# Attention then mixture of experts on one core: the first q and k turned on TensorE, later q loads in pieces between units, ten units held for the tail

## The chip, the cores and the metric

The kernel runs on one core of a Trainium2 chip. The time is the device time of one execution in microseconds (us), the median of three: 524.33 us before (523.4 to 526.0). The profile is of one further execution, whose span is 527.4 us. A core has five engines with a queue each: TensorE (PE, with its weight loads shown apart as PEld), VectorE (DVE), ScalarE (ACT), GpSimd (POOL) and SyncE (SP), which here only issues transfers. ScalarE and GpSimd issue transfers too.

## The reference

Eight sequences of 384 tokens go through multi-query attention (16 heads of 64, one shared k and v), and the result x (3072 tokens of 1024) through a mixture of 16 experts in 4 groups, where each token takes the best group and in it the best expert.

```python
scores = scale * q @ k.T                     # (8, 16, 384, 384)
attn = exp(scores - max) / sum
x = (attn @ v).transpose(0, 2, 1, 3).reshape(8 * 384, 16 * 64)
g_idx = argmax(x @ w_group); e_idx = argmax(x @ w_expert[g_idx])
out = g_w * e_w * (relu(x @ w1[g, e]) @ w2[g, e])   # g_w, e_w: softmax weights of the chosen
```

All is float32 outside; the experts' matmuls run in bfloat16. The kernel loads for each sequence the expert that most of its first 128 tokens choose, computes all 384 tokens with it, and treats tokens that chose another expert at the end, in the tail: here a single further (sequence, expert) pair, whose at most 128 tokens are gathered, computed and scattered over the output.

## The kernel before

The order of instructions on each engine is the order in the program. A step p is a third of a sequence's queries (128 rows, 16 heads); there are 24. `side` gives one of three PSUM buffers that the scores, the expert units and the small matmuls share.

```python
def load_q(b):
    t = pool.tile([P, HP, NB, 32], FP32, tag="qraw", bufs=2, name="qraw")
    for a in range(2):
        for j in range(2):
            nc.sync.dma_start(out=t[64 * a + 32 * j:64 * a + 32 * j + 32].rearrange("p h k d -> p (h k) d"), in_=qv[b, a, j].rearrange("i h k d -> i (h k) d"))
    q_raw[b] = t

def load_q_first():
    t = pool.tile([P, HP, P // 32, 32], FP32, tag="presum", bufs=2, name="qfirst")
    for k in range(P // 32):
        for a in range(2):
            for j in range(2):
                (nc.sync if a == 0 or k == 0 else nc.scalar).dma_start(out=t[64 * a + 32 * j:64 * a + 32 * j + 32, :, k], in_=qv[0, a, j, :, :, k])
    return t

def load_kv(b):
    kt = pool.tile([P, NB, 32], FP32, tag="k", bufs=1, name="k")
    for a in range(2):
        for j in range(2):
            (nc.scalar if b == 0 else nc.sync).dma_start(out=kt[64 * a + 32 * j:64 * a + 32 * j + 32], in_=kv[b, 0, j])
    k_raw[b] = kt
    vt = pool.tile([P, KB, D], FP32, tag="v", name="v")
    for c in range(2):
        (nc.gpsimd if b == 0 else nc.sync).dma_start(out=vt[64 * c:64 * c + 64], in_=v[b, 0].rearrange("(j i) d -> i j d", j=KB))
    v_sb[b] = vt
```

The first third of q is thus loaded twice: by `load_q_first` in small pieces and again with the whole of the first sequence. q and k are loaded so that a row's two halves of 32 lie on different partitions, and VectorE's 32x32 transpose finishes the turn:

```python
def prep_k(b):
    kT[b] = pool.tile([P, S], FP32, tag="kT", name="kT")
    nc.vector.transpose(out=kT[b][:], in_=k_raw[b][:].rearrange("p k d -> p (k d)"))

def q_of(p):
    b, st = divmod(p, ST)
    return q_raw[b][:, :, st * (P // 32):(st + 1) * (P // 32)].rearrange("p h k d -> p h (k d)")

def prep_q(p, src=None):
    qT[p] = pool.tile([P, 2 * CW], FP32, tag="qT", bufs=2, name="qT")
    dst = qT[p][:].rearrange("p (h n) -> p h n", h=HP)
    if src is None:
        nc.vector.transpose(out=dst, in_=q_of(p))
    else:
        for i in range(2):
            ns = slice(i * D, (i + 1) * D)
            nc.vector.transpose(out=dst[:, :, ns], in_=src[:, :, 2 * i:2 * i + 2].rearrange("p h k d -> p h (k d)"))

def scores(p, j):
    b = p // ST
    ps = side([P, 2, CW], FP32, "s")
    for c in range(2):
        for a in range(2):
            r = slice(64 * a, 64 * a + 64)
            nc.tensor.matmul(out=ps[64 * c:64 * c + 64, a, :], lhsT=kT[b][r, j * D:(j + 1) * D], rhs=qT[p][r, c * CW:(c + 1) * CW], start=True, stop=True)
    t = pool.tile([P, 2, CW], FP32, tag="pt", bufs=9, name="pt")
    nc.scalar.activation(out=t[:], in_=ps[:], func=ACTF.Exp, scale=scale)
    pt[p, j] = t
...
    def pre_add(p, j):      # sums of exponentials, VectorE
...
    def join(p):            # small matmuls: sums over keys
...
    def invert(p):          # reciprocal and spread, VectorE: rinv
...
    def weigh(p):           # xT = o * rinv on VectorE, bf16 copy on GpSimd; x_bf stored after a sequence
...
    def choose_a(b): ...    # logits of the first 128 tokens, VectorE
    def choose_b(b): ...    # counts, the expert's index, and the loads of its w1 and w2 (two buffers each)
```

The expert of a sequence is cut into 14 units that fill TensorE between the steps: 8 h units and 6 y units.

```python
    def h_unit(fc):
        if fc == 0:
            state["h"] = pool.tile([P, FO, S], BF16, tag="hT", bufs=1, name="hT")
        ps = side([P, CW], FP32, "hps")
        for ko in range(KO):
            nc.tensor.matmul(out=ps[:, 0:S], lhsT=w1[:, ko, fc * P:(fc + 1) * P], rhs=xb[:, ko, :], start=(ko == 0), stop=(ko == KO - 1))
        nc.scalar.activation(out=state["h"][:, fc, :], in_=ps[:, 0:S], func=ACTF.Relu)

    def y_unit(st, nh):
        cs = slice(nh * CW, (nh + 1) * CW)
        y = place(st, cs)
        ps = side([P, CW], FP32, "yps")
        for fo in range(FO):
            nc.tensor.matmul(out=ps[:], lhsT=state["h"][:, fo, st * P:(st + 1) * P], rhs=w2[:, fo, nh * CW:(nh + 1) * CW], start=(fo == 0), stop=(fo == FO - 1))
        nc.scalar.activation(out=y, in_=ps[:], func=ACTF.Copy, scale=gs_of()[:, st:st + 1])
        store(st, cs, y)
...
def first_units(b):
    def place(st, cs):
        y = pool.tile([P, CW], FP32, tag="y", bufs=3, name="y")
        return y[:]

    def store(st, cs, y):
        nc.sync.dma_start(out=outv[b, :, st, cs], in_=y)
    return moe_units(wts[b][0], wts[b][1], xbf[b], lambda: gsel[b], place, store)
```

The loop over the steps:

```python
def phase(n, jobs):
    for i in range(n):
        fill(1)
        if i > 0 and jobs:
            jobs.pop(0)()
    while jobs:
        jobs.pop(0)()

def jobs_choose(b):
    return [lambda: gate_a(b, 0, 1), lambda: choose_a(b), lambda: choose_b(b)]

def jobs_gate(b):
    return [lambda: gate_a(b, 1, ST), lambda: gate_math(b, gate_logits(gate_b(b))), lambda: gate_c(b)]
...
for p in range(NP):
    b, st = divmod(p, ST)
    jobs = {2: jobs_choose(0), 4: jobs_gate(0)}.get(p, [])
    for j in range(3):
        scores(p, j)
    if 0 < p < NP - 1:
        prep_q(p + 1)
    for j in range(KB):
        if p > 0:
            values(p - 1, j)
        if j == 1 and p > 0:
            join(p - 1)
        if j + 3 < KB:
            scores(p, j + 3)
        if 0 < j < 4 and jobs:
            jobs.pop(0)()
        if j > 0:
            pre_add(p, j)
        if j == 1 and p > 0:
            invert(p - 1)
        if j == 3:
            stats_q(p)
            if st == 0 and b + 1 < B:
                load_q(b + 1)
    assert not jobs
    if p == 0:
        prep_q(1)
    if p > 0:
        weigh(p - 1)
    fold_keys(p)
    if st == 1 and b + 1 < B:
        load_kv(b + 1)
    if st == 2 and b + 1 < B:
        prep_k(b + 1)
        stats_k(b + 1)
    if p > ST:
        jobs = []
        if st == 1:
            jobs = jobs_choose(b)
        if st == 0 and b > 1:
            jobs = jobs_gate(b - 1)
        if p == NP - 1:
            jobs = [bound_a, bound_b]
        phase(4 if st == 0 else 5, jobs)

    join(NP - 1)
    for j in range(KB):
        values(NP - 1, j)
    invert(NP - 1)
    weigh(NP - 1)
    fill(2)
    gate_a(last, 1, ST)
    fill(1)
    ... # gate, index of the further pair, fills between
    _, w1c, w2c, xe, ge = load_pair(pair0)      # 7 fills stand before this
    ... # gather of its tokens, 13 fills between
    while begun[0] < B or units:
        fill(1)
    ... # ph = w1c, xc -> hc (ACT); py = hc, w2c -> yc (ACT); scatter
```

Of the kernel before, what the change touches and what calls it, by code (L numbers as in the profile page):

```python
# [9 lines left out]
FP32 = mybir.dt.float32  # L10
BF16 = mybir.dt.bfloat16
I32 = mybir.dt.int32
U32 = mybir.dt.uint32
P = 128
# [7 lines left out]
def kernel(  # L22
# [11 lines left out]
    nc = tc.nc  # L34
# [7 lines left out]
    ST = S // P  # L42
# [32 lines left out]

    q_raw, k_raw, v_sb, kT, qT, pt, xT, xbf, gsel, wts = {}, {}, {}, {}, {}, {}, {}, {}, {}, {}

    def load_q(b):
        t = pool.tile([P, HP, NB, 32], FP32, tag="qraw", bufs=2, name="qraw")
        for a in range(2):  # L80
            for j in range(2):
                nc.sync.dma_start(out=t[64 * a + 32 * j:64 * a + 32 * j + 32].rearrange("p h k d -> p (h k) d"), in_=qv[b, a, j].rearrange("i h k d -> i (h k) d"))
        q_raw[b] = t

    def load_q_first():
        t = pool.tile([P, HP, P // 32, 32], FP32, tag="presum", bufs=2, name="qfirst")
        for k in range(P // 32):
            for a in range(2):
                for j in range(2):
                    (nc.sync if a == 0 or k == 0 else nc.scalar).dma_start(out=t[64 * a + 32 * j:64 * a + 32 * j + 32, :, k], in_=qv[0, a, j, :, :, k])  # L90
        return t

    def load_kv(b):
        kt = pool.tile([P, NB, 32], FP32, tag="k", bufs=1, name="k")
        for a in range(2):
            for j in range(2):
                (nc.scalar if b == 0 else nc.sync).dma_start(out=kt[64 * a + 32 * j:64 * a + 32 * j + 32], in_=kv[b, 0, j])
        k_raw[b] = kt
        vt = pool.tile([P, KB, D], FP32, tag="v", name="v")
        for c in range(2):  # L100
            (nc.gpsimd if b == 0 else nc.sync).dma_start(out=vt[64 * c:64 * c + 64], in_=v[b, 0].rearrange("(j i) d -> i j d", j=KB))
        v_sb[b] = vt

    def load_w1(w1, e):
        for a in range(2):
# [7 lines left out]
        nc.tensor.matmul(out=warm[:, 0:P], lhsT=ones_bf[:], rhs=ones_bf[:], start=True, stop=True)  # L113
    ident = singles.tile([P, P], FP32, name="ident")
    make_identity(nc, ident)
    load_kv(0)
    q_first = load_q_first()
    load_q(0)

    one = singles.tile([P, 1], FP32, name="one")  # L120
    nc.vector.memset(one[:], 1.0)
    iota16 = singles.tile([P, GE], FP32, name="iota16")
    nc.gpsimd.iota(iota16[:], pattern=[[1, GE]], base=0, channel_multiplier=0, allow_small_or_imprecise_dtypes=True)
    iota128 = singles.tile([P, NPAIR], FP32, name="iota128")
# [45 lines left out]

    def stats_k(b):
        junk = pool.tile([P, 2 * CW], BF16, tag="junk", bufs=1, name="junk")
        nc.scalar.activation(out=junk[:, 0:S], in_=k_raw[b][:].rearrange("p k d -> p (k d)"), func=ACTF.Square, accum_out=stat_k[:, b:b + 1])

    def prep_k(b):
        kT[b] = pool.tile([P, S], FP32, tag="kT", name="kT")
        nc.vector.transpose(out=kT[b][:], in_=k_raw[b][:].rearrange("p k d -> p (k d)"))

    def q_of(p):
        b, st = divmod(p, ST)  # L180
        return q_raw[b][:, :, st * (P // 32):(st + 1) * (P // 32)].rearrange("p h k d -> p h (k d)")

    def prep_q(p, src=None):
        qT[p] = pool.tile([P, 2 * CW], FP32, tag="qT", bufs=2, name="qT")
        dst = qT[p][:].rearrange("p (h n) -> p h n", h=HP)
        if src is None:
            nc.vector.transpose(out=dst, in_=q_of(p))  # L187
        else:
            for i in range(2):
                ns = slice(i * D, (i + 1) * D)  # L190
                nc.vector.transpose(out=dst[:, :, ns], in_=src[:, :, 2 * i:2 * i + 2].rearrange("p h k d -> p h (k d)"))

    def scores(p, j):
        b = p // ST
# [10 lines left out]

    def pre_add(p, j):
        if j == 1:
            presum[p] = pool.tile([P, 2, CW], FP32, tag="presum", bufs=2, name="presum")
            nc.vector.tensor_add(out=presum[p][:], in0=pt[p, 0][:], in1=pt[p, 1][:])  # L209
        else:  # L210
            nc.vector.tensor_add(out=presum[p][:], in0=presum[p][:], in1=pt[p, j][:])  # L211
# [133 lines left out]
    def moe_units(w1, w2, xb, gs_of, place, store):  # L345
# [24 lines left out]
                units.append(lambda st=st, nh=nh: y_unit(st, nh))  # L370
        return units

    def first_units(b):
        def place(st, cs):
            y = pool.tile([P, CW], FP32, tag="y", bufs=3, name="y")
            return y[:]

        def store(st, cs, y):
            nc.sync.dma_start(out=outv[b, :, st, cs], in_=y)
        return moe_units(wts[b][0], wts[b][1], xbf[b], lambda: gsel[b], place, store)  # L380

    NP = B * ST

    prep_k(0)
    for _ in range(36):
        nc.tensor.matmul(out=warm[:, 0:P], lhsT=ones_bf[:], rhs=ones_bf[:], start=True, stop=True)
    prep_q(0, q_first)
    load_gw()
    stats_k(0)

    units = []
    begun = [0]
# [1 line left out]
    def fill(n):  # L394
        while n > 0:
            if not units:
                if begun[0] >= B or begun[0] not in wts:
                    return
                units.extend(first_units(begun[0]))
                begun[0] += 1  # L400
            units.pop(0)()
            n -= 1

    def phase(n, jobs):
        for i in range(n):
            fill(1)
            if i > 0 and jobs:
                jobs.pop(0)()
        while jobs:
# [7 lines that stand above are left out]
# [10 lines left out]
    def bound_b():  # L427
# [9 lines left out]
        nc.vector.tensor_copy(out=oki[:], in_=okf[:])  # L437
        bound["okf"] = okf

    for p in range(NP):  # L440
        b, st = divmod(p, ST)
        jobs = {2: jobs_choose(0), 4: jobs_gate(0)}.get(p, [])
        for j in range(3):
            scores(p, j)
        if 0 < p < NP - 1:
            prep_q(p + 1)
        for j in range(KB):
            if p > 0:
                values(p - 1, j)
            if j == 1 and p > 0:  # L450
                join(p - 1)
            if j + 3 < KB:
                scores(p, j + 3)
            if 0 < j < 4 and jobs:
                jobs.pop(0)()
            if j > 0:
                pre_add(p, j)
            if j == 1 and p > 0:
                invert(p - 1)
            if j == 3:  # L460
                stats_q(p)
                if st == 0 and b + 1 < B:
                    load_q(b + 1)
        assert not jobs
        if p == 0:
            prep_q(1)
        if p > 0:
            weigh(p - 1)
        fold_keys(p)
        if st == 1 and b + 1 < B:  # L470
            load_kv(b + 1)
        if st == 2 and b + 1 < B:
            prep_k(b + 1)
            stats_k(b + 1)
# [5 lines that stand above are left out]
                jobs = jobs_gate(b - 1)  # L480
            if p == NP - 1:
                jobs = [bound_a, bound_b]
            phase(4 if st == 0 else 5, jobs)

    join(NP - 1)
    for j in range(KB):
        values(NP - 1, j)
# [32 lines left out]
    def load_pair(pair):  # L520
        e_reg = nc.s_assert_within(pair & (GE - 1), 0, GE - 1, skip_runtime_bounds_check_because="the bits of an index below 128")
        b_reg = nc.s_assert_within(pair >> 4, 0, B - 1, skip_runtime_bounds_check_because="the bits of an index below 128")
        xe = pool.tile([P, KO, S], BF16, tag="xbf", bufs=3, name="xe")
        nc.sync.dma_start(out=xe[:].rearrange("p k s -> p (k s)"), in_=xb_dram[bass.ds(b_reg, 1)].rearrange("a p k -> (a p) k"))
        w1 = wpool.tile([P, KO, F], BF16, tag="w1", name="w1")
        load_w1(w1, e_reg)
        w2 = wpool.tile([P, FO, Dm], BF16, tag="w2", name="w2")
        nc.gpsimd.dma_start(out=w2[:], in_=w2f[bass.ds(e_reg, 1)].rearrange("a p k f -> (a p) k f"))
        ge = pool.tile([P, ST], FP32, tag="gsel", bufs=4, name="ge")
        nc.vector.tensor_copy(out=ge[:], in_=gate_all[:, bass.ds(pair, 1), :].rearrange("p a s -> p (a s)"))  # L530
        return b_reg, w1, w2, xe, ge
# [108 lines left out]
    with rare_block:  # L640
# [7 lines left out]
      with tc.If(ok < 1):  # L648
# [4 lines left out]
          with tc.For_i(0, B * H, 1) as i:  # L653
# [13 lines left out]
              for qt in range(ST):  # L667
# [2 lines left out]
                  sm1 = pool.tile([P, 4], FP32, tag="sm1", bufs=2, name="sm1")  # L670
                  nc.vector.reduce_max(out=sm1[:, 0:1], in_=sp[:, 0, 0:S], axis=AX)
                  nc.vector.tensor_scalar(out=sm1[:, 1:2], in0=sm1[:, 0:1], scalar1=-scale, scalar2=None, op0=OP.mult)
                  at = pool.tile([P, S], FP32, tag="presum", bufs=2, name="at")
                  nc.scalar.activation(out=at[:], in_=sp[:, 0, 0:S], func=ACTF.Exp, bias=sm1[:, 1:2], scale=scale)
                  nc.vector.reduce_sum(out=sm1[:, 2:3], in_=at[:], axis=AX)
                  nc.vector.reciprocal(out=sm1[:, 3:4], in_=sm1[:, 2:3])
# [58 lines left out]
```

## Time and profile before

| what | value |
|---|---|
| time, median of 3 | 524.33 us (523.4 to 526.0) |
| span of the profiled execution | 527.4 us |
| mean granted TensorE clock | 0.959 of full |
| scores (L199): 1152 matmuls, busy | 151.5 us |
| values (L240): 1152 matmuls, busy | 142.5 us |
| h units (L354) and y units (L362), busy | 89.6 and 87.1 us |
| transfers of q (L82) | 32 of 384 KB, median 8.5 us from issue to landing |
| stores of y (L379) | 48 of 256 KB, median 4.5 us |
| weight loads: half of w1 and w2, in POOL's queue | 1024 KB 11.6 us, 2048 KB 24.9 us |

In the timeline a row gives the start in us, the length, the engine, the line, the operation with its tiles and how many were merged; in brackets is the idle time of that engine just before, and what ended it. An engine name with q (SPq) is its queue, which issues a transfer. A wait line gives: the engine and line that waited, for which engine and line, us in total, how many times, the longest.

### The profile page before, as it was taken

To read this page: it belongs to the slowest core of one execution; us is meant where nothing else is said; L and a number is where in the kernel's file an instruction comes from. 1 tells how busy PE (TensorE), PEld (TensorE's weight loads), DVE (VectorE), ACT (ScalarE), POOL (GpSimd) and SP (SyncE) were. 2 spreads that over 40 slices of the span, in tenths; PEclk is the share of its full clock that TensorE was granted. 3 is DMA by queue.
4 is the path that set the end of the run, shared out by engine and by line. 5 is a ranking of instruction groups with operands and counts; after the bars stand their busy time and mean duration, and the time that the engine had idled before them with its cause. 6 is when DMAs were issued, how large, how long until landed. Compare 5 with 4: busy or idle time off the path is not lost. (4 is left out here: it accounts for less than half of the span.)

```text
span 527.4 us, 9497 instructions
## 1 busy us (share of the span) xinstructions
PE 476.6 (90%) x3915; PEld 205.4 (39%) x3939; DVE 312.3 (59%) x490; ACT 247.2 (47%) x349; POOL 49.3 (9%) x66
## 2 busy tenths in 40 slices
PE   5598697999899979999899979999999999999943
PEld 4132233344244334344244334344344344445531
DVE  3668587657657747657567647657756765725110
ACT  1555352654554544654545634653655564423211
POOL 2001100100020000100020000100020002001000
PEclk8789798999999989999899999999999999999986
DMA  9893995699429990799419991799349431984980
GB/s 120 76 132 50 189 199 113 116 221 161 152 35 204 193 201 20 127 225 159 139 23 205 193 204 28 131 226 188 107 66 202 107 127 23 207 229 120 231 191 11
DMA packets 154210, 74.52 MB, mean 141 GB/s; under 512 B 128347, under 2 KB 128347, under 8 KB 154160
## 3 DMA queue, kind: packets, MB, share of 16 engines
q0 software_dynamic: 19104, 38.03, 39.9%
q1 hardware_dynamic: 131824, 35.42, 36.6%
q10 hardware_dynamic: 3232, 0.39, 0.5%
q8 instruction: 33, 0.54, 0.4%
q14 instruction: 17, 0.14, 0.1%
HBM read 92.62 MB, written 19.40 MB: 212 GB/s over the span
## 5 line engine op out<-in xcount | busy, mean ns | idle before, releaser
L201 ACT ACTIVATE pt<-s 128x1024 f32<-128x1024 f32 x144 | 142.7, 1025 | 81.1 <-PE s L199 80.9
L199 PE MATMUL s<-qT,kT 64*64 64x512 f32 x1152 | 151.5, 627 | 27.4 <-ACT y L363 10.9
L240 PE MATMUL o<-pt,v 64*64 64x512 f32 x1152 | 142.5, 596 | 0.4 <-DVE xT L248 0.4
L211 DVE TENSOR_TENSOR presum<-presum,pt 128x1024 f32<-128x1024 f32 x96 | 116.7, 1215 | 7.3
L354 PE MATMUL hps<-xbf,w 128*128 128x384 bf16 x512 | 89.6, 329 | 0.0
L362 PE MATMUL yps<-w,hT 128*128 128x512 bf16 x361 | 87.1, 380 | 1.2
L199 PEld LDWEIGHTS s<-qT,kT 64*64 64x64 f32 x1152 | 41.1, 140 | 96.6 <-issue 63.1
L209 DVE TENSOR_TENSOR presum<-pt 128x1024 f32<-128x1024 f32 x24 | 29.3, 1222 | 76.6 <-ACT pt L201 76.6
L240 PEld LDWEIGHTS o<-pt,v 64*64 64x64 f32 x1152 | 43.6, 135 | 79.6 <-issue 75.1
L363 ACT ACTIVATE y<-yps,gsel 128x512 f32<-128x512 f32 x48 | 33.0, 687 | 85.0 <-PE yps L362 58.5
L354 PEld LDWEIGHTS <-w 128*128 128x128 bf16 x512 | 47.9, 100 | 42.1 <-issue 13.8
L355 ACT ACTIVATE hT<-hps 128x384 bf16<-128x384 f32 x64 | 31.4, 490 | 68.9 <-PE hps L354 60.2
L249 POOL CAST xbf<-xT 128x1024 bf16<-128x1024 f32 x24 | 25.0, 1040 | 381.5 <-DVE xT L248 381.5
L362 PEld LDWEIGHTS <-hT 128*128 128x128 bf16 x384 | 36.4, 99 | 47.3 <-issue 8.6
L248 DVE TENSOR_TENSOR xT<-o,rinv 128x1024 f32<-128x1024 f32 x24 | 29.2, 1218 | 3.6 <-PE o L240 3.6
L230 DVE STREAM_TRANSPOSE rinv<-rc 128x1024 f32<-128x1024 f32 x24 | 29.9, 1245 | 0.8
L215 DVE TRANSPOSE_TENSOR_REDUCE fold<-presum 128x32 f32<-128x1024 f32 x24 | 29.6, 1233 | 0.0
L187 DVE STREAM_TRANSPOSE qT<-qraw 128x1024 f32<-128x1024 f32 x23 | 28.1, 1223 | 0.0
L228 DVE RECIPROCAL rc<-sm 128x32 f32<-128x32 f32 x24 | 8.5, 356 | 29.5 <-PE sm L223 29.5
L169 ACT ACTIVATE junk<-qraw 128x1024 bf16<-128x1024 f32 x24 | 25.2, 1048 | 0.2 <-DMA qraw<-in_q_dram 0.2
L261 PE MATMUL gps<-xT,gw 128*32 128x128 f32 (+1 forms) x256 | 14.2, 340 | 4.4 <-DVE xT L248 4.4
L304 DVE COPY L<-lps 128x60 f32<-128x60 f32 x8 | 1.8, 220 | 27.1 <-PE lps L269 27.1
(135 smaller groups left out, 181.2 us busy)
## 6 DMA issues: line engine op xcount, KB each, us to landing
w<-in_moe_w_dram POOLq DMA_DIRECT2D x18, 1024.0 KB, 11.6
w<-in_moe_w_dram POOLq DMA_DIRECT2D x9, 2048.0 KB, 24.9
qraw<-in_q_dram SPq DMA_DIRECT2D x32, 384.0 KB, 8.5
out_dram<-y SPq DMA_DIRECT2D x48, 256.0 KB, 4.5
x_bf<-xbf SPq DMA_DIRECT2D x8, 768.0 KB, 6.8
k<-in_k_dram SPq DMA_DIRECT2D x28, 48.0 KB, 2.4
v<-in_v_dram SPq DMA_DIRECT2D x14, 96.0 KB, 2.6
xe<-x_bf SPq DMA_DIRECT2D x1, 768.0 KB, 4.5
```

The lines of the kernel that those rows point to most:

```text
L199: nc.tensor.matmul(out=ps[64 * c:64 * c + 64, a, :], lhsT=kT[b][r, j * D:(j + 1) * D], rhs=qT[p][r, c * CW:(c + 1) * CW], start=True, stop ...
L201: nc.scalar.activation(out=t[:], in_=ps[:], func=ACTF.Exp, scale=scale)
L209: nc.vector.tensor_add(out=presum[p][:], in0=pt[p, 0][:], in1=pt[p, 1][:])
L211: nc.vector.tensor_add(out=presum[p][:], in0=presum[p][:], in1=pt[p, j][:])
L215: nc.vector.tensor_reduce(out=fold[p][:], in_=presum[p][:].rearrange("p a (n i) -> p (a n) i", i=32), axis=AX, op=OP.add, apply_transpose= ...
L230: nc.vector.transpose(out=t[:].rearrange("p (b i) -> p b i", i=32), in_=rc[:].rearrange("p c b -> p (c b)").unsqueeze(2).to_broadcast([P, ...
L240: nc.tensor.matmul(out=o_ps[p][64 * a:64 * a + 64, c, :], lhsT=v_sb[b][r, j, :], rhs=pt[p, j][r, a, :], start=(j == 0), stop=(j == KB - 1))
L248: nc.vector.tensor_mul(out=xT[b][:, :, ts], in0=o_ps[p][:].rearrange("p c (h n) -> p (c h) n", n=P), in1=rinv[p][:].rearrange("p (h n) -> ...
L354: nc.tensor.matmul(out=ps[:, 0:S], lhsT=w1[:, ko, fc * P:(fc + 1) * P], rhs=xb[:, ko, :], start=(ko == 0), stop=(ko == KO - 1))
L355: nc.scalar.activation(out=state["h"][:, fc, :], in_=ps[:, 0:S], func=ACTF.Relu)
L362: nc.tensor.matmul(out=ps[:], lhsT=state["h"][:, fo, st * P:(st + 1) * P], rhs=w2[:, fo, nh * CW:(nh + 1) * CW], start=(fo == 0), stop=(fo ...
L363: nc.scalar.activation(out=y, in_=ps[:], func=ACTF.Copy, scale=gs_of()[:, st:st + 1])
```

## The change

It touches three places.

The first sequence's q and k are loaded in their natural layout, token rows on partitions, two heads side by side (each k row twice), and turned by TensorE against the identity into PSUM, from where ScalarE and VectorE copy them. The second load of the first third goes. A dummy exponential makes ScalarE load its table early. This is for an earlier first score and for step 1 to follow at once.

Later sequences' q come in eight pieces of 192 KB, one after each unit, so that other transfers in SyncE's queue need not stand behind the whole of q. y gets a fourth buffer (in the tail it takes one of the nine buffers of the exponentials), presum one instead of two, xe moves to q's buffers. In the early steps the jobs of the choice and the gate stand ahead of the values, and `join` and `invert` one j later.

The steps get 4 or 5 units by a list, 88 in all where it was 94, so that ten units of the seventh sequence and all 14 of the eighth are left for the tail, where TensorE has the small gate work and the weights of the further pair to wait for.

```diff
     def load_q(b):
         t = pool.tile([P, HP, NB, 32], FP32, tag="qraw", bufs=2, name="qraw")
-        for a in range(2):
-            for j in range(2):
-                nc.sync.dma_start(out=t[64 * a + 32 * j:...], in_=qv[b, a, j]...)
         q_raw[b] = t
+        n = HP // 2
+        def piece(i, a, j):
+            hs = slice(i * n, (i + 1) * n)
+            nc.sync.dma_start(out=t[64 * a + 32 * j:..., hs]..., in_=qv[b, a, j, :, hs]...)
+        for i in range(2):
+            for a in range(2):
+                for j in range(2):
+                    q_todo.append(lambda i=i, a=a, j=j: piece(i, a, j))
...
+    def load_first():
+        kt = pool.tile([P, ST, 2, D], FP32, tag="k", bufs=1, name="kn")
+        qt = pool.tile([P, ST, HP, 2, D], FP32, tag="qraw", bufs=2, name="qn")
+        for a in range(2):
+            nc.scalar.dma_start(out=kt[:, :, a], in_=kn)
+        for c in range(2):
+            hs = slice(c * HC, (c + 1) * HC)
+            for a in range(2):
+                nc.sync.dma_start(out=qt[:, 0, hs, a], in_=qn[0, :, a, hs])
+        load_v(0)
+        for st in range(1, ST):
+            for a in range(2):
+                nc.sync.dma_start(out=qt[:, st, :, a], in_=qn[st, :, a])
...
+    nc.scalar.activation(out=wake[:], in_=one[:], func=ACTF.Exp)
...
+    def turn_k_first(): ...  # 3 PE transposes, one VectorE copy
+    def turn_q_first(st, copies):
+        ps = side([P, 2, CW], FP32, "qps")
+        for hp in range(HP):
+            nc.tensor.transpose(out=ps[:, hp // HC, ...], in_=q_raw[0][:, st, hp]..., identity=ident[:])
+        ... # copied out in len(copies) parts
...
-            presum[p] = pool.tile([P, 2, CW], FP32, tag="presum", bufs=2, name="presum")
+            presum[p] = pool.tile([P, 2, CW], FP32, tag="presum", bufs=1, name="presum")
...
-            y = pool.tile([P, CW], FP32, tag="y", bufs=3, name="y")
+            if done[0]:
+                y = pool.tile([P, 2 * CW], FP32, tag="pt", bufs=9, name="yt")
+            else:
+                y = pool.tile([P, CW], FP32, tag="y", bufs=4, name="y")
...
-    prep_k(0)
     for _ in range(36):
         nc.tensor.matmul(out=warm[:, 0:P], ...)
-    prep_q(0, q_first)
+    turn_k_first()
+    turn_q_first(0, [nc.scalar.copy, nc.vector.tensor_copy])
     load_gw()
-    stats_k(0)
...
     def phase(n, jobs):
         for i in range(n):
             fill(1)
+            some_q()
...
+    FIVES = (4, 6, 8, 10, 13, 15, 17, 20)
     for p in range(NP):
+        if st == 0 and b + 1 < B:
+            load_q(b + 1)
         for j in range(3):
             scores(p, j)
-        if 0 < p < NP - 1:
+        if p == 0:
+            turn_q_first(1, [nc.vector.tensor_copy])
+            stats_k(0)
+        elif p == 1:
+            turn_q_first(2, [nc.scalar.copy])
+        elif p < NP - 1:
             prep_q(p + 1)
         for j in range(KB):
+            if jobs:
+                jobs.pop(0)()
             if p > 0:
                 values(p - 1, j)
-            if j == 1 and p > 0:
+            if j == 2 and p > 0:
                 join(p - 1)
             if j + 3 < KB:
                 scores(p, j + 3)
-            if 0 < j < 4 and jobs:
-                jobs.pop(0)()
             if j > 0:
                 pre_add(p, j)
-            if j == 1 and p > 0:
+            if j == 2 and p > 0:
                 invert(p - 1)
             if j == 3:
                 stats_q(p)
-                if st == 0 and b + 1 < B:
-                    load_q(b + 1)
+            if p < 4 and 0 < j < 5:
+                some_q()
...
-            phase(4 if st == 0 else 5, jobs)
+            phase(5 if p in FIVES else 4, jobs)
+    done[0] = True
...
-        xe = pool.tile([P, KO, S], BF16, tag="xbf", bufs=3, name="xe")
+        xe = pool.tile([P, KO, S], BF16, tag="qraw", bufs=2, name="xe")
```

## The prediction

> **What bounds the kernel now.** I read the busy line first, then the idle time of TensorE in order of time, then the waits of the engines at each hole. The chain that ended last reaches back only to the final scatter (7 us), so it says nothing on the 520 us before it.
>
> ```profile
> PE 476.6 (90%) x3915; PEld 205.4 (39%) x3939; DVE 312.3 (59%) x490; ACT 247.2 (47%) x349; POOL 49.3 (9%) x66
> PEclk8789798999999989999899999999999999999986
> ```
>
> TensorE is busy 90% of a 527.4 us span; VectorE and ScalarE have over 200 us free each. So the time is PE work plus PE holes plus work done at half clock. The timeline of TensorE shows where the holes are (start, length, what, idle before it and who ended it):
>
> ```profile
> 12.52 7.33 PE L199 MATMUL s<-qT,kT 64*64 64x512 f32 x48 [4.99 <-DVE qT L191]
> 25.18 5.25 PE L199 MATMUL s<-qT,kT 64*64 64x512 f32 x24 [5.33 <-DVE qT L187]
> 38.09 2.76 PE L199 MATMUL s<-qT,kT 64*64 64x512 f32 x24
> 56.78 4.81 PE L199 MATMUL s<-qT,kT 64*64 64x512 f32 x24 [6.13 <-DVE kT L177]
> 88.83 1.08 PE L261 MATMUL gps<-xT,gw 128*32 128x128 f32 x16 [3.30 <-DVE xT L248]
> 135.90 1.09 PE L199 MATMUL s<-qT,kT 64*64 64x512 f32 x8 [1.75 <-ACT y L363]
> 194.66 1.99 PE L199 MATMUL s<-qT,kT 64*64 64x512 f32 x8 [2.91 <-ACT y L363]
> 254.19 1.09 PE L199 MATMUL s<-qT,kT 64*64 64x512 f32 x8 [2.33 <-ACT y L363]
> 314.48 1.09 PE L199 MATMUL s<-qT,kT 64*64 64x512 f32 x8 [2.73 <-ACT y L363]
> 371.53 1.09 PE L199 MATMUL s<-qT,kT 64*64 64x512 f32 x8 [1.20 <-ACT y L363]
> 503.74 3.73 PE L625 MATMUL ph<-xc,w 128*128 128x128 bf16 x64 [1.76 <-DVEq L640]
> 513.01 0.59 PE L631 MATMUL py<-w,hc 128*128 128x512 bf16 x1 [5.54 <-DMA w<-in_moe_w_dram]
> ```
>
> Three families: the start (4.99, 5.33, 6.13, 3.30), a hole per batch behind y (1.75 to 2.91, sum 10.92), the tail (1.76, 5.54). The same 24 score matmuls last 2.76 us, or 4.81 and 5.25 after a long hole: each long hole also costs about 2 us of half clock. The waits name what lies behind the y holes and the tail:
>
> ```profile
> ACT y L363 <- DMA out_dram<-y: 25.2, 8, 4.6
> PE py L631 <- DMA w<-in_moe_w_dram: 5.5, 1, 5.5
> ```
>
> ScalarE cannot write y because its three buffers await their stores; in the SyncE timeline those stores stand behind the q load:
>
> ```profile
> 114.18 13.27 SPq L82 DMA_DIRECT2D qraw<-in_q_dram  x4
> 127.54 3.09 SPq L251 DMA_DIRECT2D x_bf<-xbf  x1
> 130.73 5.47 SPq L379 DMA_DIRECT2D out_dram<-y  x4
> ```
>
> The four q issues hold the queue 13.27 us, then x_bf, and the first y of the group goes out only at 130.73.
>
> **What the Trainium skill says.** "TensorE: Matmul & The Clock Gate", Part 1 (the HAM clock gate): an idle window of about 3.4 us halves the clock, and about as long a busy stretch restores it. The trace agrees: 6.13 us idle gave 4.81 us for work that otherwise takes 2.76, 2.33 us idle gave none (1.09 for 8). The same page, Part 4 (PE-mode transpose): PE turns a full 128x128 block, the result goes to PSUM and needs a copy, and such work does not count as busy for the clock. No such float32 turn of data runs in the kernel before. "DMA: Bandwidth & Descriptors", "Why small descriptors are slow (HBM only)": each packet has a fixed cost. The trace agrees: 4 x 384 KB of q in 128-byte runs took 13.27 us to issue, 118 GB/s, while the whole span reaches 229 in its best slices. "ScalarE: Activation LUTs", "What ACT_TABLE_LOAD costs": about 1.28 us; the trace has 1.28 at 8.34.
>
> **The change part by part.** I call p the attention step (batch x third of the sequence), 24 in all.
>
> *Start, p=0 and p=1.* Before, scores began at 12.52 and p=1's at 25.18, because the first q came in 16 small loads and then once more whole, and p=1 waited for that second load. Now each row is one 256-byte run, the first third comes in 4 loads and nothing is loaded twice. Issues cost about 0.65 us each on SyncE (6.45 for 10), so the first third is issued by 3.7 us and lands near 7 (2.5 to 3.4 us landing for such small loads in the list of issues). PE's warm-up ends at 7.5. Then 3 turns of k and 8 of q. I estimate a float32 turn at 0.25 us from the 128x128 float32 weight loads (0.85 us for 6) plus 128 columns of moving data (1.07 us for 4 rounds of 256 columns, so 0.13): 2.8 us for 11. Half-row copies of about 0.65 us end near 10.7. First score 10.5 to 11, a gain of 1.7. The exponentials (1.02 us each) then pace the step: from 11.5, six and the square of k, with the 8 turns of p=1 (2 us) and a 1.2 us copy inside them. Scores of p=1 start near 17 against 25.18. In p=1, PE does 10.3 us of scores and values (96 matmuls at 0.107, the pace of 24 in 2.6) + 2.0 turns + small, 13.2: p=2 begins at 30.2 against 38.09. **Gain 7.9**, of which 2.4 is half clock.
>
> *p=2 to p=5.* p=2 lasted 18.7 us (38.09 to 56.78), VectorE-bound: its chain of choice work waited 1.73 us for gate logits in the middle of the sums, and the k turn stood at its end. Now the choice jobs stand before the first sum, where VectorE awaited the exponentials anyhow. VectorE's work from the first sum: 5 sums x 1.22 + inverse 1.6 + counts 0.6 + xT 1.2 + fold 1.2 + kT 0.55 = 11.3, starting 3.3 after the step: 14.6, plus perhaps 0.4 as the second batch's q lands near 31. **Gain 3.7**; the hole shrinks from 6.1 to about 3, so p=3 may keep part of its half clock: **0.5**. The hole of 3.30 and its slow 1.08 + 2.32 (for 0.43 + 1.46) come from the same lag one step on, with the gate jobs of p=4 moved forward too: of 4.8, **3**.
>
> *The y holes.* A fourth y buffer, units spread differently (a batch's y now run 1 to 5 to a step), and q issues of 192 KB between stores instead of four in a row. Stores then wait for one piece (about 1.7 us) and x_bf. Steady cycles of three steps took 58.6 us with a hole of 2.73, 57.05 with 1.20, and 55.6 with none, so a hole costs its length plus about 0.2. **Gain 11 to 12**, all five holes.
>
> *Ten units.* 94 units stood in the loop and 18 in the tail; now 88 and 24. The moved six are 4 h (1.36) + 2 y (1.8): 9 us of PE work from before the tail's weight load to after it. Seven units still stand before the load, so it is issued 9 us earlier relative to PE's work. Before, w2 came 30 us after the first issue (482.91 to 513.0) while PE was ready near 508. Three or four more y stores (256 KB, at some 230 GB/s 1.1 us each) now run beside the load: w2 at about 30 + 3.5, or 507.5 on the old clock, and PE arrives at 506 (the 1.76 hole is filled by the last four units). Gain 5.5, and py at full clock: 16 x 0.43 = 6.9 becomes 3.8: 3.1. **Gain 8**, less if stores delay w2.
>
> *Cost.* Taking units from the steps shortens them: p=11 has 4 h (5.4 us) instead of 3 h + 2 y (7.5). There k's turn ended 3.0 us before PE needed it; this leaves about 0.5, as the later inverse adds 0.5 on VectorE. And the last q pieces of a batch are issued in the very step before they are turned, behind y stores, landing some 4 us into the step where VectorE used to start its sums at 3.1. VectorE idles 1.7 us later in the chain, which absorbs most of it. **Loss about 2**.
>
> Sum: 7.9 + 3.7 + 0.5 + 3 + 11.5 + 8 - 2 = 32.6, so 491.7. I take 493, since overlapping gains rarely come whole.
>
> **Rivals.** (1) *Late q pieces bind VectorE and so PE.* For: the order of issues on SyncE puts the last 2 to 4 pieces of each batch behind a y store, and slack at kT falls to about 0.5 us. Against: the 1.7 us idle and 5-unit steps at p=8, 17, 20. If each of six batches lost 2.5 us, the total is about 505. (2) *The tail load is hidden anyway or grows.* The weight transfer could be slowed by the stores moved beside it, or w2 held back because three y units of the same buffer stand after the load. Against: w1 occupies the transfer first for half of the 30 us. If true, 8 becomes 2 and the total 498. (3) *Cold start.* If turning keeps PE cold, p=0 and p=1 run at half clock: 4 us lost, total 496. (4) *The y holes stay*, because the stores are slow for weight traffic and not for queueing (their landing median is 4.5 us, up to 7.6): half the gain, 498.
>
> **Range and chances.** One rival alone gives 496 to 505; two together about 509. If all terms hold and the loss of 2 does not come, 489; a start that gains 3 more gives 486. So 484 to 506 in 8 of 10. For less than 2% (above 513.8) more than 20 of the 32 would have to vanish, and the terms lie in three separate places: chance of faster 0.92, within 2% 0.06, slower 0.02.
>
> **What would show it.** First score near 10.7, p=1 at 17, p=2 at 30; the k hole of batch 1 at most 3 us; no PE idle on y; py starting within 2 us of hc with 16 matmuls in 4 us. Wrong if PE shows repeated holes on kT or qT at every third step, if VectorE waits on qraw, or if py still waits over 4 us on w.

## The result and the profile after

The changed kernel takes 493.98 us (491.87 to 495.05, four executions) against 525.16 us for the kernel before beside it: a ratio of 0.939, with a 95% interval of 0.933 to 0.946. The prediction was 493, between 484 and 506. The two profiled executions, 527.4 and 490.4 us, lie 37.0 us apart, somewhat more than the medians (31.2); the account by stages below is of these two.

The busy line and the granted clock of the page of the kernel after:

```profile
PE 467.3 (95%) x3944; PEld 206.8 (42%) x3966; DVE 310.3 (63%) x488; ACT 248.6 (51%) x352; POOL 48.0 (10%) x64
PEclk9999999999999999999999999999999999999998
```

TensorE is now busy 95% of the span instead of 90%, and the clock's digits no longer dip, though the first scores of step 3 still run partly slow (4.22 us below, against 2.75 for the same 24 matmuls in step 2). The timeline of TensorE, kernel after (start, length, what; in brackets the idle time just before and who ended it):

```profile
9.15 3.52 PE L237 MATMUL s<-qT,kT 64*64 64x512 f32 x24 [0.68 <-ACT qT L215]
13.63 5.38 PE L237 MATMUL s<-qT,kT 64*64 64x512 f32 x48
28.55 2.75 PE L237 MATMUL s<-qT,kT 64*64 64x512 f32 x24
47.18 4.22 PE L237 MATMUL s<-qT,kT 64*64 64x512 f32 x24 [5.61 <-DVE kT L219]
62.53 1.07 PE L299 MATMUL gps<-xT,gw 128*32 128x256 f32 x16 [0.71 <-DVE xT L286]
78.31 0.65 PE L299 MATMUL gps<-xT,gw 128*32 128x128 f32 x16 [2.21 <-DVE xT L286]
475.47 3.74 PE L676 MATMUL ph<-xc,w 128*128 128x128 bf16 x64
479.04 3.62 PE L682 MATMUL py<-w,hc 128*128 128x512 bf16 x15
```

Of the eleven holes of before two are left, 5.61 before step 3 and 2.21 in step 4; the first of before is now 0.68, and a new small one of 0.71 stands at 62.53. Nothing after the first 80 us is longer than 0.6 us. No line names y any more, and py follows ph at once and at full clock (15 recorded matmuls in 3.62 us).

By stages, with the starts of the same work in both traces (step 4's scores start at 69.27 before and 59.08 after, step 5's at 94.86 and 83.06):

| stage | before | after | gained | predicted |
|---|---|---|---|---|
| start to scores of step 2 | 38.09 | 28.55 | 9.5 | 7.9 |
| step 2 | 18.69 | 18.63 | 0.1 | 3.7 |
| step 3 | 12.49 | 11.90 | 0.6 | 0.5 |
| steps 4 to scores of step 5 | 25.59 | 23.98 | 1.6 | 3 |
| step 5 to the last join (462.22; 427.40) | 367.36 | 344.34 | 14.0 | 11.5 - 2 |
| last join to end | 65.2 | 63.0 | 11.2 | 8 |

In the last two rows the six moved units are allowed for: 4 h at 1.36 and 2 y at 1.81 are 9.06 us that left one row and entered the other (367.36 - 344.34 - 9.06 = 14.0; 65.2 - 63.0 + 9.06 = 11.2). The sum is 37.0, where the prediction had 32.6.

What took the place of the q load on SyncE, in its timeline of the kernel after:

```profile
114.28 0.36 SPq L289 DMA_DIRECT2D x_bf<-xbf  x1
114.74 0.38 SPq L422 DMA_DIRECT2D out_dram<-y  x1
115.22 0.87 SPq L87 DMA_DIRECT2D qraw<-in_q_dram  x1
116.17 1.42 SPq L422 DMA_DIRECT2D out_dram<-y  x1
117.65 0.46 SPq L87 DMA_DIRECT2D qraw<-in_q_dram  x1
```

A y store now waits for x_bf or one piece of q, not for 13.27 us of q.

### The profile page after: what moved, and what is told of

Same layout as the page of the kernel before. It is cut to its first block, busy times and chain, and to the rows that moved or that the text cites. A ratio compares the mean times of both kernels' runs of the same rounds, so it can differ in the third digit from the quotient of the medians.

```text
span 490.4 us, 9586 instructions
## 1 busy us (share of the span) xinstructions
PE 467.3 (95%) x3944; PEld 206.8 (42%) x3966; DVE 310.3 (63%) x488; ACT 248.6 (51%) x352; POOL 48.0 (10%) x64
## 5 line engine op out<-in xcount | busy, mean ns | idle before, releaser
L237 PE MATMUL s<-qT,kT 64*64 64x512 f32 x1152 | 144.4, 601 | 6.8 <-DVE kT L219 5.6
L278 PE MATMUL o<-pt,v 64*64 64x512 f32 x1152 | 140.8, 590 | 0.0
L401 ACT ACTIVATE y<-yps,gsel 128x512 f32<-128x512 f32 x36 | 24.8, 688 | 49.2 <-PE yps L400 37.5
L229 DVE STREAM_TRANSPOSE qT<-qraw 128x1024 f32<-128x1024 f32 x21 | 25.7, 1224 | 15.2 <-DMA qraw<-in_q_dram 10.6
L194 ACT ACTIVATE junk<-qraw 128x1024 bf16<-128x1024 f32 x21 | 22.0, 1048 | 0.0
L131 POOL DMA_DIRECT2D w<-in_moe_w_dram x18 | 12.6, 706 | 51.2 <-PE s L237 19.4
```

What stands on the lines that cost most here:

```text
L229: nc.vector.transpose(out=qT[p][:].rearrange("p (h n) -> p h n", h=HP), in_=q_of(p))
L278: nc.tensor.matmul(out=o_ps[p][64 * a:64 * a + 64, c, :], lhsT=v_sb[b][r, j, :], rhs=pt[p, j][r, a, :], start=(j == 0), stop=(j == KB - 1))
```

## The experiments

Each ratio is to the kernel before, run beside it. The changed kernel itself, run once more with more rounds, serves as the base: 

> The changed kernel itself, as the base for the two beside it: 492 to 495.

 It took 493.97 us, ratio 0.935 (0.931 to 0.939). Per hundredth of ratio that is some 5.3 us. Beside the three groups of runs below the kernel before took 528.69, 528.62 and 527.94 us, so that their times compare with this base.

**The tail: 94 units in the loop again.** My theory was that the ten units held back hide the wait for w2; the rival, that the larger choice of y buffers in the tail did it.

```diff
-            phase(5 if p in FIVES else 4, jobs)
+            phase(4 if st == 0 else 5, jobs)
```

> The changed kernel with 94 units in the loop again, 18 in the tail. Theory (the units held back hide the wait for the further pair's w2, and py then runs at full clock): PE idle of 4 to 6 us before py comes back, 16 matmuls of py take near 6.9 instead of 3.6 us, the hole of about 1.8 before ph too; the time is 8 to 11 us above the changed kernel (493.98), so 502 to 505. Rival (what was gained in the tail comes from the y buffers taken from the exponentials' nine, not from the units): within 3 us of the changed kernel.

It took 505.69 us, ratio 0.958 (0.951 to 0.965), 11.7 us more than the base. TensorE's timeline of this run:

```profile
480.09 3.73 PE L676 MATMUL ph<-xc,w 128*128 128x128 bf16 x64 [1.76 <-DVEq L691]
489.59 0.59 PE L682 MATMUL py<-w,hc 128*128 128x512 bf16 x1 [5.76 <-DMA w<-in_moe_w_dram]
490.40 5.50 PE L682 MATMUL py<-w,hc 128*128 128x512 bf16 x14 [0.22 <-issue]
```

Both holes and the half clock return as they were before, although y still has the nine buffers: the rival falls. 1.76 + 5.76 + the 2.7 us by which py is slower (489.59 to 495.90 is 6.31, against 3.62) make 10.2 of the 11.7. The old spread of the units also brings more holes of 0.57 us at the matmuls of the logits (six against two), which may account for the rest.

**The y holes: fourth buffer, pieces, or spread?** Three kernels: three y buffers; q's pieces issued in a row at the old place; both.

```diff
-                y = pool.tile([P, CW], FP32, tag="y", bufs=4, name="y")
+                y = pool.tile([P, CW], FP32, tag="y", bufs=3, name="y")
```

```diff
-        if st == 0 and b + 1 < B:
-            load_q(b + 1)
...
             if j == 3:
                 stats_q(p)
+                if st == 0 and b + 1 < B:
+                    load_q(b + 1)
+                    some_q(8)
```

Three buffers alone: 

> The changed kernel with three y buffers instead of four, q still in pieces. Theory (stores no longer stand behind the whole q load, which was the cause): no PE hole behind y longer than 1 us, time within 2 us of 494. Rival (the fourth buffer did it): holes of 1.5 to 3 us at four or more batches, time 8 to 12 us longer, 502 to 506.

 Measured 493.11 us, 0.935 (0.928 to 0.941), no hole behind y.

Pieces in a row alone: 

> The changed kernel with all eight q pieces issued in a row where the kernel before issued q, four y buffers. Theory (queueing behind q was the cause): ScalarE waits for y stores return, but with four buffers and at most four y units in a row the wait is partly covered: PE holes sum 3 to 8 us, time 497 to 502. Rival (fourth buffer did it): time within 2 us of 494.

 Measured 494.30 us, 0.937 (0.930 to 0.945); ScalarE waited once for a store, 2.6 us, and TensorE once for y, 0.48 us. I had expected holes of 3 to 8 us in sum here, and missed: the rival, that the fourth buffer did it, is what came.

Both: 

> Both undone: three y buffers and q in a row. Theory and rival alike: the y holes are back, sum 8 to 11 us plus 2 of half clock, time 503 to 507. A third view (the new spread of the units over the steps did it, neither buffer nor pieces): within 3 us of 494.

 Measured 505.78 us, 0.957 (0.950 to 0.964). SyncE, ScalarE and TensorE in this run:

```profile
111.99 5.94 SPq L87 DMA_DIRECT2D qraw<-in_q_dram  x4
118.03 1.30 SPq L289 DMA_DIRECT2D x_bf<-xbf  x1
119.45 6.40 SPq L422 DMA_DIRECT2D out_dram<-y  x5
124.18 1.31 ACT L401 ACTIVATE y<-yps,gsel 128x512 f32<-128x512 f32 x2 [4.79 <-DMA out_dram<-y]
124.92 1.95 PE L237 MATMUL s<-qT,kT 64*64 64x512 f32 x16 [2.21 <-ACT y L401]
183.74 1.09 PE L237 MATMUL s<-qT,kT 64*64 64x512 f32 x8 [3.46 <-ACT y L401]
```

The first y, ready at 113.8 (113.10 + 0.69 in ScalarE's timeline), is stored from 119.45, and the fourth write waits for it. The holes behind y are 2.21, 3.46, 2.29 and 0.66 us, 8.6 in sum, and two of them are followed by half clock (1.7 us each, worked out as for the kernel before in the next part): 12.0, against the 11.8 by which this run is slower than the base. So the theory (queueing) and the rival (buffers) are both half right: the holes need late stores and too few buffers at once, and either remedy alone removes them. The spread of the units alone does not: it is in this kernel too. The kernel before bears this out with the buffer alone (presum gives up its second buffer for the room):

```diff
-            y = pool.tile([P, CW], FP32, tag="y", bufs=3, name="y")
+            y = pool.tile([P, CW], FP32, tag="y", bufs=4, name="y")
```

> The kernel before with a fourth y buffer as its only gain (presum takes one buffer instead of two to make room). Theory (either the fourth buffer or the pieces suffice for the y holes): the five holes of 1.2 to 2.9 us go, ratio to the kernel before 0.975 to 0.982 (9 to 13 us). Rival (with two y units following four others in the old spread, four buffers do not reach, the spread is needed): under 4 us.

It took 513.93 us, 0.972 (0.969 to 0.976), 14.7 us less than the 528.62 beside it, a little more than expected: a single buffer brings the whole of this part (14.0 in the account by stages). Its timeline has no hole behind y; those of the start (5.81, 4.88, 6.13, 3.31) and of the tail (1.76, 5.89) each lie within 0.9 us of before.

**The start: the old loads and turns in the changed kernel.**

```diff
-    load_first()
+    load_kv0()
+    q_first = load_q_first()
+    load_q0()
...
+    prep_k(0)
...
-    turn_k_first()
-    turn_q_first(0, [nc.scalar.copy, nc.vector.tensor_copy])
+    prep_q(0, q_first)
...
-        if p == 0:
-            turn_q_first(1, [nc.vector.tensor_copy])
-            stats_k(0)
-        elif p == 1:
-            turn_q_first(2, [nc.scalar.copy])
-        elif p < NP - 1:
+        if 0 < p < NP - 1:
             prep_q(p + 1)
...
+        if p == 0:
+            prep_q(1)
```

> The changed kernel with the first q and k loaded and turned as before (small loads, then the whole again; VectorE transposes), all else kept. Theory (the new load alone brought scores of step 2 from 38.1 to 28.6 us): step 2 begins near 38, time 9 to 12 us longer, 503 to 506. Rival (VectorE bounds steps 1 to 3 anyhow, so an earlier start is absorbed there): the hole before step 3 shrinks by several us and the time is only 3 to 6 us longer.

504.04 us (500.90 to 504.26; a fourth execution, 514.11, was in the core's slower state and is left out), 0.951 (0.945 to 0.957): 10.1 us above the base by the medians, 8.4 by the ratios. Its TensorE timeline (the view ends at 60 us, so that its last row has 16 of the 24 matmuls; all 24 took 5.26):

```profile
12.57 7.92 PE L269 MATMUL s<-qT,kT 64*64 64x512 f32 x48 [6.08 <-DVE qT L261]
25.56 5.40 PE L269 MATMUL s<-qT,kT 64*64 64x512 f32 x24 [5.07 <-DVE qT L257]
57.10 3.69 PE L269 MATMUL s<-qT,kT 64*64 64x512 f32 x16 [5.07 <-DVE kT L247]
```

The start is that of before (step 2 begins at 38.89), and the hole before step 3 is hardly smaller (5.07 against 5.61). The rival, that VectorE would absorb it, falls. The run undoes loads and turns together, so what each is worth stays open.

**The place of the jobs.** Step 2 gained nothing although the choice jobs moved forward in it. This kernel puts jobs, join and invert back:

```diff
         for j in range(KB):
-            if jobs:
-                jobs.pop(0)()
             if p > 0:
                 values(p - 1, j)
-            if j == 2 and p > 0:
+            if j == 1 and p > 0:
                 join(p - 1)
             if j + 3 < KB:
                 scores(p, j + 3)
+            if 0 < j < 4 and jobs:
+                jobs.pop(0)()
```

> The changed kernel with the choice and gate jobs of steps 2 and 4, join and invert back at their old places. Theory (VectorE enters step 2 some 4 us behind, so that where the jobs stand in the step changes nothing there): the hole before step 3 stays at 5 to 7 us, step 3 begins within 1 us of 47.2, and only the hole of 2.2 us in step 4 grows to about 3.3; time 1 to 3 us longer, 495 to 497. Rival (the prediction's step: the new place is worth 3.7 us in step 2 and 3 in steps 4 and 5): 5 to 7 us longer, 499 to 501.

494.12 us, 0.935 (0.931 to 0.938): no different from the base, and just under the 495 to 497 expected; the rival's 499 to 501 did not come. The holes were 6.23 and 3.31 us instead of 5.61 and 2.21, as the theory had them. So the new place is worth a microsecond or two of holes at most, which the times don't resolve.

**VectorE's queue in step 2.** The trace of the kernel after, VectorE alone, shows what stands between the start of step 2 (28.55) and k's turn (a selection of rows):

```profile
30.64 1.22 DVE L286 TENSOR_TENSOR xT<-o,rinv 128x1024 f32<-128x1024 f32 x1
31.78 1.24 DVE L253 TRANSPOSE_TENSOR_REDUCE fold<-presum 128x32 f32<-128x1024 f32 x1
32.94 1.20 DVE L229 STREAM_TRANSPOSE qT<-qraw 128x1024 f32<-128x1024 f32 x1
35.59 1.22 DVE L247 TENSOR_TENSOR presum<-pt 128x1024 f32<-128x1024 f32 x1
44.30 1.22 DVE L286 TENSOR_TENSOR xT<-o,rinv 128x1024 f32<-128x1024 f32 x1
45.43 1.23 DVE L253 TRANSPOSE_TENSOR_REDUCE fold<-presum 128x32 f32<-128x1024 f32 x1
46.59 0.54 DVE L219 STREAM_TRANSPOSE kT<-k 128x384 f32<-128x384 f32 x1
```

VectorE ends step 1 at 33.0, 4.5 us into step 2, and the first sum starts at 35.59, 7.0 us into it, not 3.3 as I had it. Before, the same fold ended at 42.16, 4.1 us into step 2, and the first sum started at 43.22, 5.1 us into it. Two ways to test what binds. First, less work for VectorE: the first sum of steps 1 to 4 on GpSimd.

```diff
-            nc.vector.tensor_add(out=presum[p][:], in0=pt[p, 0][:], in1=pt[p, 1][:])
+            (nc.gpsimd if 1 <= p <= 4 else nc.vector).tensor_add(out=presum[p][:], in0=pt[p, 0][:], in1=pt[p, 1][:])
```

> The changed kernel with the first sum of exponentials of steps 1 to 4 (four adds of 128 x 1024) on GpSimd instead of VectorE. Theory (VectorE's work in steps 1 and 2 sets when k of the second batch is turned): the hole of 5.6 us before step 3 shrinks by about 1.2 us per add moved ahead of it, to 3 to 3.5, part of the half clock after it goes, and the hole of 2.2 us in step 4 goes to under 1; time 4 to 6 us shorter, 488 to 490. Rival (the choice's chain from PE to VectorE and back sets it, or an add on GpSimd takes so long that VectorE waits for it): hole over 5 us, time within 2 us of 494.

492.08 us, 0.931 (0.928 to 0.935), the same as the base within the noise, and the hole 5.19: the theory missed, and what the rival said came. GpSimd and VectorE in this run:

```profile
22.61 2.37 POOL L247 TENSOR_TENSOR presum<-pt 128x1024 f32<-128x1024 f32 x1 [20.34 <-DVE fold L253]
25.01 1.23 DVE L249 TENSOR_TENSOR presum<-presum,pt 128x1024 f32<-128x1024 f32 x1 [2.55 <-POOL presum L247]
```

The add takes 2.37 us there, 1.9 times VectorE's 1.23 (the Trainium skill, "GPSIMD Engine Reference", section 3.1 on elementwise work, has 1.96 for a float32 add of another size: the trace agrees, and I had not allowed for it), could not start before the fold of the previous step had freed the only presum buffer, and VectorE waited 2.55 us for it. So it took little off the path and decides nothing on the theory.

Second, the same work in another order: k's turn from the end of the step to its middle.

```diff
             if j == 3:
                 stats_q(p)
+                if st == 2 and b + 1 < B:
+                    prep_k(b + 1)
...
         if st == 2 and b + 1 < B:
-            prep_k(b + 1)
             stats_k(b + 1)
```

> The changed kernel with the VectorE turn of the next batch's k moved from the end of every third step (behind the last sums, xT and fold) to its middle, behind the third sum; no work is taken away. Theory A (the hole of 5.6 us before step 3 is the place of that turn at the end of VectorE's queue, and VectorE has idle time in step 3 to catch up): the hole shrinks to under 1 us, a smaller one of 1 to 2 us shows at the values (waiting for xT), no half clock in step 3, time 3.5 to 5.5 us shorter. Theory B (VectorE's total work in steps 1 to 4 is the bound): the hole only moves a step on, as a longer wait for xT, and the time stays within 1.5 us.

487.13 us, 0.922 (0.919 to 0.926), 6.8 us under the base beside it, more than the 3.5 to 5.5 expected. VectorE and TensorE in this run:

```profile
41.95 0.57 DVE L219 STREAM_TRANSPOSE kT<-k 128x384 f32<-128x384 f32 x1
42.58 2.81 PE L237 MATMUL s<-qT,kT 64*64 64x512 f32 x24 [0.28 <-DVE kT L219]
44.87 1.22 DVE L286 TENSOR_TENSOR xT<-o,rinv 128x1024 f32<-128x1024 f32 x1
46.14 1.09 PE L278 MATMUL o<-pt,v 64*64 64x512 f32 x8 [0.76 <-DVE xT L286]
```

The hole of 5.61 us becomes 0.28 at the scores and 0.76 at the values, which wait for xT, and step 3's scores run at full clock (2.81 instead of 4.22). Theory A holds: what held step 3 back was one 0.57 us instruction behind two sums, xT and fold (2.51 + 1.22 + 1.24 us here), which TensorE needed later or not yet, and not the amount of VectorE's work. The sum fits: in the base beside it the hole was 5.60 and the slow scores took 5.39, so 5.60 + (5.39 - 2.81) - 0.28 - 0.76 makes 7.1 of holes and clock, where the time fell by 6.8.

Last, with work for TensorE in the hole of step 4 as well:

```diff
-    def phase(n, jobs):
+    def phase(n, jobs, after=0):
         for i in range(n):
             fill(1)
             some_q()
-            if i > 0 and jobs:
+            if i > after and jobs:
                 jobs.pop(0)()
...
-            phase(5 if p in FIVES else 4, jobs)
+            phase(5 if p in FIVES else 4, jobs, 2 if p == 4 else 0)
```

> As the one before, and the choice of step 4 begins after four units instead of two, so that PE has work while VectorE finishes xT. Theory A: the hole of 2.2 us in step 4 goes, another 1 to 2 us, in all 5 to 7 us shorter. Theory B: VectorE is still the bound and the hole returns at the scores of step 5 or their qT, no more than 0.5 us gained.

484.87 us (484.24 to 485.47), 0.918 (0.914 to 0.922): 9.1 us under the changed kernel beside it, more than the expected 5 to 7 and 2.3 us under the run before, and the fastest version here. The 2.21 us hole is gone; a 0.90 us one at the choice's counts is what shows in its place.

```profile
76.38 0.18 PE L326 MATMUL c1ps<-ohe,ones_bf 128*128 128x16 bf16 x1 [0.90 <-DVE ohe L321]
```

## Why the prediction was right

Each of the three places, undone by itself, costs about what was predicted of it or more: the start 10.1 us, the y holes 11.8, the tail 11.7, by medians against the base, each uncertain by 3 to 4 us. They add up to 33.6, and the whole change brings 31 to 34, so that they are independent as far as the noise tells. The sum was right for the stated reasons in these three places, with the following terms off:

- **Start, predicted 7.9, measured 9.5.** The step "a float32 turn at 0.25 us" was mis-sized: eight turns show as 1.04 to 1.09 us, 0.13 each, so that the first eleven end 1.4 us sooner than the 2.8 worked out. The first score came at 9.15, not 10.7, and step 2 began at 28.55, not 30.2. The cold start of rival 3 did not come; the clock was full from the first slice, though two microseconds of turns are too few to say whether turning counts as busy for it.
- **Step 2, predicted 3.7, measured 0.1. This step failed.** I had VectorE begin its sums 3.3 us after the step, as if it came to the step idle and the choice would fill a wait. In both traces it is still finishing step 1 for over 4 us of step 2, so the choice put ahead of the first sum only delayed that sum (7.0 us into the step instead of 5.1), and k's turn at the end came no earlier (18.0 us into the step; 18.1 before). The k hole that was to be at most 3 us was 5.61. The experiment with k's turn in the middle shows where the gain had been: in the order of VectorE's queue.
- **Steps 4 and 5, predicted 3, measured 1.6.** The hole went from 3.30 to 2.21, which is 1.1; the slow clock after it went, which is 1.3 (0.65 and 1.47 us now for what took 1.08 and 2.32); the new hole at 62.53 took 0.7 back. Of the prediction's working, "0.43" for the first of these should have been 0.65, so there were 4.6 us to gain and not 4.8.
- **The y holes, predicted 11.5, measured 14.0** with the predicted loss of 2 not seen. The term that was mis-sized is "its length plus about 0.2": two of the five holes also brought half clock. The prediction read "2.33 us idle gave none (1.09 for 8)" from the first eight matmuls alone. The kernel before went slow a microsecond later, and after the longer hole of 2.73 it did not:

```profile
254.19 1.09 PE L199 MATMUL s<-qT,kT 64*64 64x512 f32 x8 [2.33 <-ACT y L363]
255.10 1.60 PE L240 MATMUL o<-pt,v 64*64 64x512 f32 x8
256.47 1.95 PE L199 MATMUL s<-qT,kT 64*64 64x512 f32 x8
258.17 1.38 PE L240 MATMUL o<-pt,v 64*64 64x512 f32 x8
314.48 1.09 PE L199 MATMUL s<-qT,kT 64*64 64x512 f32 x8 [2.73 <-ACT y L363]
315.38 1.04 PE L240 MATMUL o<-pt,v 64*64 64x512 f32 x8
316.24 1.04 PE L199 MATMUL s<-qT,kT 64*64 64x512 f32 x8
```

  From the end of the hole to the next join, the same work took 3.48 us after the holes of 1.75, 2.73 and 1.20, but 5.18 after that of 2.33 and 4.83 after that of 2.91. That is 1.70 and 1.35 more, and 10.92 + 3.05 makes the 14.0. The cycles of 58.6 and 57.05 us, from which the 0.2 came, are two without half clock. That "stores then wait for one piece" is what the queue shows, but it is not what was needed: the fourth buffer would have done.
- **The tail, predicted 8, measured 11.2.** The hole of 5.54 went as worked out. The 1.76 hole went too: it was named but not summed, because py was still to wait some 1.5 us for w2, and it did not; the stores moved beside the load did not make w2 late. py itself gained 2.6 and not 3.1 (6.19 us before, from 513.01 to 519.20, and 3.62 now). These three are 9.9; the remaining 1.3 is not accounted for.
- **The loss of 2** was half right. The late pieces do hold VectorE in the kernel after, three times, by up to 4.69 us. That was named as a sign of being wrong, and it came:

```profile
196.53 1.25 DVE L229 STREAM_TRANSPOSE qT<-qraw 128x1024 f32<-128x1024 f32 x1 [3.70 <-DMA qraw<-in_q_dram]
251.60 1.25 DVE L229 STREAM_TRANSPOSE qT<-qraw 128x1024 f32<-128x1024 f32 x1 [4.69 <-DMA qraw<-in_q_dram]
```

Yet no hole at kT or qT follows in TensorE after step 3. That VectorE's idle time later in the chain takes it up, as the prediction argued, was not tested.

The errors went both ways: 5.0 us too much in steps 2, 4 and 5, 9.4 too little elsewhere. That the single number lies only 1 us off owes something to this, and to the medians lying closer together than the two profiled executions.

## What to carry to other kernels

When TensorE waits on another engine, look at what stands ahead of the awaited instruction in that engine's queue: moving one short instruction forward was worth 6.8 us here, while rearranging the work ahead of it, or giving some of it to a slower engine, changed the hole by 0.6 us or less. Where a buffer waits for its store, count buffers and queue together: one more buffer did as much as splitting the transfers ahead of it, and both together no more. Filler work held back for a stage that waits on a transfer earned twice here: 7.5 us of holes, and 2.7 us because the work after the wait then ran at full clock. So when you price a hole, look at the clock for several microseconds behind it, and not only at the first matmuls.

## What I had not expected of the hardware

A float32 128 x 128 turn on TensorE costs 0.13 us in a row of eight, about half of what I had taken from weight load plus moving data: the two overlap (for the first eight turns of q, weight loads from 7.33 to 8.24 and matmuls from 7.44 to 8.48). And the length of a hole alone does not tell whether the clock falls, nor do the first matmuls after it. Holes of 2.33 and 2.91 us in the kernel before were followed by half clock, one of 2.73 was not; so the idle window of 3.4 us that the prediction went by does not hold for these. After the hole of 2.33, and after 3.46 and 2.29 in the run with both y remedies undone, the first eight score matmuls still took 1.09 us, and the slow stretch began about one microsecond later (1.95 us for eight) and cost 1.7.
